# Two decoder layers on one core: other places for the scratch, for w1 and w2 between the layers, and for the kept quarters of V and K

## The chip, the core and the metric

The kernel runs on one core of one Trainium2 chip. TensorE multiplies matrices into PSUM, VectorE, ScalarE and GpSimd work element by element, and SyncE issues the transfers from HBM to SBUF. The metric is the device time of one launch in microseconds. Seen from the profiler, the span runs from the first to the last instruction; the time of the same execution holds a little more.

## The reference

Two times in turn, an attention layer and an MLP are applied to one token x of 512 numbers, with the same weights and the same cache both times:

```
x = x + attention(layernorm(x))     # q = x @ wq, 32 heads of 128, 4096 cached keys and values each
x = x + gelu(layernorm(x) @ w1 + b1) @ w2 + b2      # 512 -> 1376 -> 512, tanh form of gelu
```

All is float32. The scores are q k / sqrt(128), then a softmax over 4096 positions, then the sum of the values, and wo brings 4096 numbers back to 512. K and V take 67 MB each, so nearly all the time's traffic is K and V, read once for each layer.

## The kernel before

**Groups and blocks.** Four heads at a time make a group; there are G = 8 groups, called heads below where the code counts g or n. One group's K, or its V, is a block of 8 MB: 128 partitions x 8 chunks (C) of NC = 2048 numbers, a chunk being four quarters of U = 512. Layer one goes through g = 0 to 7; layer two goes back from g = 7 to 0 (n = 0 to 7), because the last blocks of layer one are still in SBUF when it starts: K and V of g = 7 whole, V of g = 6 in part.

**SBUF.** One tensor, arena, holds everything large, and the code places each piece by its first column:

- Three homes of a whole block each, at A_AT = 0, C_AT = 8 NC and B_AT = 16 NC. In layer one block number 2g (K) and 2g + 1 (V) takes home A, B, C in turn. In layer two, from n = 2 on, the order of homes is A, C, B.
- SHARED, which begins inside home B behind the kept quarters of V (26 of 32) and reaches beyond it: wq at the start, w1 and w2 between the layers, and some of K at the start of layer two.
- SCRATCH, one quarter: the exponentials p of a head, and in head_out the turned copy of the values' sums (ot).
- PAIR, two chunks: wo of this group and wq of the next.

**One head.** scores (64 products of 128 x 512 into pS, one block of K), exponentials (maximum, then ScalarE's exp into SCRATCH), weights (four transposes of p by TensorE, L208, and the denominators), values (64 products into pO, one block of V), head_out (VectorE's transpose L227 into SCRATCH, the reduction L231 that reads it, then the product with wo), next_queries (the product with wq of the next group). The group's share of the attention output is added up in acc.

**Kept quarters.** At g = 6 the last six quarters of V are copied to the PSUM banks pK0 to pK5 by ScalarE as they are used; the other 26 stay in home B. In layer two they are copied back, two to the end of home C and four to PAIR, once those places are free, and V of g = 6 isn't loaded again. K of g = 6 is loaded again in pieces (begin_k), into SHARED, PAIR and home C as they come free.

**Order.** load() puts every transfer on SyncE and keeps it in program order, as matmul() does on TensorE. VectorE, ScalarE and GpSimd are ordered by the tile framework. The framework also adds the waits: an instruction that writes a region of arena waits for those ahead of it in the program that read or wrote an overlapping region. A load so waits on SyncE, and the loads behind it wait with it. A load takes one of eight semaphores in turn, so it also waits for the load eight places ahead of it.

**Between the layers.** The last head of layer one loads its V in four pieces (LAST), then wo, three columns of w1, and behind head_out the fourth. mlp multiplies the four columns into pO, and loads w2 (11 blocks of a quarter) in four pieces as places come free; idle() issues products of zeros that add nothing to the result. Then first_queries begins layer two.

**After that** each head of layer two loads its K, its V (that of n = 2 as five and three chunks) and its pair of weights.

The lines that the change touches:

Of the kernel before, what the change touches and what calls it, by code (L numbers as in the profile page):

```python
# [17 lines left out]
P = 128  # L18
# [3 lines left out]
G = 8  # L22
J = 4
C = 8
FJ = F // J
FB = 11
W1C = FJ * J
EPS = 1e-5
U = 512
# [3 lines left out]

RING = (0, 16 * NC, 8 * NC)
A_AT, B_AT, C_AT = RING
KEPT_V = 26 * U
SHARED = B_AT + KEPT_V
SCRATCH = SHARED + 10 * U  # L40
PAIR = SHARED + 11 * U
ARENA = PAIR + 2 * NC
HALVES = ((0, 4), (4, 8))
W1_AT_END = ((0, 2), (2, 3), (3, 4))
LAST = ((0, 4), (4, 6), (6, 7), (7, 8))
W2_AT_CHANGE = ((0, 2), (2, 5), (5, 8), (8, 11))
W2_AT_END = ((0, 4), (4, 8), (8, 10), (10, 11))


# [1 line left out]
def decode_layers(ctx: ExitStack, tc: tile.TileContext, x, k, v, w, w1, b1, w2, b2, out):  # L51
# [13 lines left out]
    def at(first, n):  # L65
        return arena[:, first : first + n]
# [6 lines left out]
    def matmul(*a, **kw):  # L73
        tc.keep_in_program_order(nc.tensor.matmul(*a, **kw))  # L74
# [53 lines left out]
    def pairs(t):  # L128
        return t[:, :8].rearrange("p (c i) -> p c i", i=2)
# [27 lines left out]
    def minus_mean(s, at):  # L157
        for j in range(J):
            matmul(at[32 * j : 32 * j + 32, :], negmean, s, start=True, stop=True)
        return at  # L160

    def mean_of(xs, s):
        nm = minus_mean(s, pS[:, 0:1])
        xc, sq, ss, negm = small("xc", 4), small("sq", 4), small("ss"), small("negm")
        nc.vector.tensor_scalar(xc, pairs(xs)[:, :, 0], nm, None, op0=ALU.add)
        nc.vector.scalar_tensor_tensor(sq, xc, 1.0, xc, op0=ALU.mult, op1=ALU.mult, accum_out=ss)
        nc.vector.tensor_copy(negm, nm)
        return negm, ss

    def rstd_of(ss):  # L170
        nv = minus_mean(ss, pS[:, 1:2])
        ve, r = small("ve"), small("rstd")
        nc.vector.tensor_scalar(ve, nv, -1.0, EPS, op0=ALU.mult, op1=ALU.add)
        nc.vector.memset(pS[:, 0:2], 0.0)
        nc.gpsimd.tensor_tensor(r, ve, power, op=ALU.pow)
        return r

# [44 lines left out]
            matmul(pO[32 * j : 32 * j + 4, :], pt[:, j, c, :], vt[j],  # L222
                   start=(i == 0), stop=(i == C - 1))

    def head_out(rl, wt, last=False):
        ot = at(SCRATCH, U)
        nc.vector.transpose(ot, pO)  # L227
        o, on = small("o", 4), on_wide
        own = at(SCRATCH, 4 * 129).rearrange("p (b q) -> p b q", q=129)[:, :, :P]
        own = own.rearrange("p b (d q) -> p d b q", q=32)[:, :, :, 0]  # L230
        nc.vector.tensor_reduce(o, own, axis=AX.X, op=ALU.add)  # L231
        if last:
            nc.vector.tensor_scalar(on[:, :4], o, rl, None, op0=ALU.mult)
        else:
            nc.vector.tensor_scalar(in_quarters(on, 4), o.unsqueeze(1).to_broadcast([P, J, 4]), rl, None,  # L235
                                    op0=ALU.mult)
        for d in range(4):
            if last:
                for j in range(J):
                    matmul(pS[32 * j : 32 * j + 1, :P], on[:, d : d + 1], wt[:, d, P * j : P * (j + 1)],  # L240
                           start=(d == 0), stop=(d == 3))
            else:
                matmul(pO, on[:, d : d + P], wt[:, d, :], start=(d == 0), stop=(d == 3))
        return of_32(turned(pS) if last else turned(pO, wide=True), 4)

    def mlp(xs, s, w1_t, w2_t, load_w2=None):
        xb = small("xb", 4)
        nc.gpsimd.tensor_tensor(xb, pairs(xs)[:, :, 0], b2c, op=ALU.add)  # L248
        for c in range(4):
            for j in range(J):  # L250
                matmul(pO[32 * j : 32 * j + 2, :FJ], pairs(xs)[:, c, :], w1_t[c][:, FJ * j : FJ * (j + 1)],
                       start=(c == 0), stop=(c == 3))
            if c == 0:
                nm, ss = mean_of(xs, s)
            if c == 1:
                r = rstd_of(ss)
            if load_w2 and c < 3:
                load_w2(c)
        idle(pS)
        ht = at(SCRATCH, 32 * FB)  # L260
        nc.vector.transpose(ht, pO[:, : 32 * FB])
        h, u, a, z, t, g = (small(f"gelu_{i}", FB) for i in "huaztg")
        nc.vector.scalar_tensor_tensor(h, of_32(ht, FB, 1), nm, of_32(ht, FB), op0=ALU.mult, op1=ALU.add)
        if load_w2:
            load_w2(3)
        nc.vector.scalar_tensor_tensor(u, h, r, b1c, op0=ALU.mult, op1=ALU.add)
        nc.vector.scalar_tensor_tensor(a, u, 0.044715, u, op0=ALU.mult, op1=ALU.mult)
        nc.vector.scalar_tensor_tensor(z, a, 1.0, u, op0=ALU.add, op1=ALU.mult)
        nc.scalar.activation(t, z, AF.Tanh, scale=float(np.sqrt(2.0 / np.pi)))
        nc.vector.scalar_tensor_tensor(g, t, 1.0, u, op0=ALU.add, op1=ALU.mult)  # L270
        for c in range(FB):
            for j in range(J):
                matmul(pS[32 * j : 32 * j + 1, :P], g[:, c : c + 1], w2_t[c][:, P * j : P * (j + 1)],
                       start=(c == 0), stop=(c == FB - 1))
            if load_w2 and any(c == b - 1 for a, b in W2_AT_CHANGE):
                idle(pO)
        return of_32(turned(pS), 4), xb

    def load_w1(first, a, b):
# [33 lines left out]
    def add_up(acc, own):  # L313
        t = small("acc", 4)
        nc.vector.scalar_tensor_tensor(t, own, 1.0, acc, op0=ALU.mult, op1=ALU.add)
        return t


    negm, z, sc, nsc = first_queries(xs, s, wq_t)
    acc = pairs(xs)[:, :, 0]  # L320
    for g in range(G):
        final = g == G - 1
        k_home, v_home = RING[2 * g % 3], RING[(2 * g + 1) % 3]
        for c, t in blocks(k, g, k_home, HALVES if final else ((0, C),)):
            scores(z, c, t)
        pt, rl = weights(exponentials(sc, nsc))
        for c, t in blocks(v, g, v_home, LAST if final else ((0, C),)):
            values(c, pt, t, c)
            if final and c > 4:
                idle(pS)  # L330
            if g == G - 2:
                for j in range(J):
                    i = 4 * c + j - KEPT_V // U
                    if i >= 0:
                        nc.scalar.copy(pK[i], t[j])
        if final:
            wo_t = by_four(load(PAIR, of_w(g % 2, g, 1)))
            for i in range(3):
                load_w1(SHARED, i, i + 1)
            own = head_out(rl, wo_t, last=True)  # L340
            load_w1(SHARED, 3, 4)
        else:
            pair = load(PAIR, of_w(g % 2, g, 2))
            acc = add_up(acc, head_out(rl, by_four(pair[:, :NC])))
            wq_t = by_four(pair[:, NC:])
            z = next_queries(g + 1, xs, negm, wq_t)
    x1, s1 = set_x(own, 1.0, acc, queries=False)
    own, xb = mlp(x1, s1, in_rows(SHARED, W1C, 4), in_rows(SHARED, U, FB),
                  lambda i: load_w2(SHARED, *W2_AT_CHANGE[i]))
    xs, s = set_x(own, 0.5, xb)  # L350


# [2 lines left out]
    g = G - 2  # L355
    negm, z, sc, nsc = first_queries(xs, s, wq_t)
    acc = pairs(xs)[:, :, 0]
    wq_t = by_four(load(SHARED, of_w((g + 1) % 2, g, 1)))
    k_t = []

    def begin_k(home, n):
# [1 line left out]
        load(home, k[g][:, U * a : U * (a + n)])  # L363
        k_t.extend(at(home + U * i, U) for i in range(n))

    begin_k(SHARED + NC, 4)
    begin_k(SHARED + 2 * NC, 2)
    begin_k(PAIR + NC, 4)
    for c in range(C):
        scores(z, c, quarters(C_AT + NC * c))  # L370
# [1 line left out]
            begin_k(C_AT + NC * c, 4)  # L372
        if c == 5:
            begin_k(C_AT + 2 * NC, 14)
    pair = load(C_AT + 22 * U, of_w(g % 2, g - 1, 2))
    p = exponentials(sc, nsc)
    z = next_queries(1, xs, negm, wq_t)
    pt, rl = weights(p)
# [1 line left out]
        values(c, pt, quarters(A_AT + NC * c), c)  # L380
    acc = add_up(acc, head_out(rl, wo_t))

    v_t = [at(B_AT + U * i, U) for i in range(KEPT_V // U)]
    for i, first in enumerate([C_AT + 30 * U, C_AT + 31 * U] + [PAIR + U * j for j in range(4)]):
        t = at(first, U)
        nc.scalar.copy(t, pK[i])
        v_t.append(t)
    for c in range(C):
        scores(z, c, k_t[4 * c : 4 * c + 4])
    pt, rl = weights(exponentials(sc, nsc))  # L390
# [6 lines left out]
    for n in range(2, G):  # L397
        g, final = G - 1 - n, n == G - 1
        k_home, v_home = homes[(2 * n - 1) % 3], homes[2 * n % 3]
        for c, t in blocks(k, g, k_home, HALVES if final else ((0, C),)):  # L400
            scores(z, c, t)
        pt, rl = weights(exponentials(sc, nsc))
        for c, t in blocks(v, g, v_home, LAST if final else ((0, 5), (5, 8)) if n == 2 else ((0, C),)):
            values(c, pt, t, c)
            if final and c > 4:
                idle(pS)
        if final:
            wo_t = by_four(load(PAIR, of_w(g % 2, g, 1)))
            for a, b in W1_AT_END:
                load_w1(A_AT, a, b)  # L410
            for a, b in W2_AT_END:
                load_w2(A_AT + 11 * U, a, b)
            own = head_out(rl, wo_t, last=True)
        else:
            pair = load(PAIR, of_w(g % 2, g - 1, 2))
            acc = add_up(acc, head_out(rl, by_four(pair[:, NC:])))
            z = next_queries(n + 1, xs, negm, by_four(pair[:, :NC]))
# [47 lines left out]
```

## Time and profile before

| | |
|---|---|
| Median of 3 runs | 680.82 us (680.7 to 681.85) |
| Profiled execution, time | 679.55 us |
| Profiled execution, span | 677.8 us |
| Mean granted clock of TensorE | 0.841 |
| Read from HBM | 286.14 MB, 422 GB/s over the span |
| TensorE products, busy | 433.1 us (64%) |
| VectorE, busy | 110.7 us (16%) |
| ScalarE, busy | 22.2 us (3%) |
| GpSimd, busy | 4.3 us (1%) |

In the profile, PE is TensorE, DVE VectorE, ACT ScalarE, POOL GpSimd, SPq the list of SyncE, which is never counted as busy. L74 is the line of matmul(), L70 that of load(), so groups there are told apart by the names behind them: pS<-arena,zq are scores, pO<-arena,turned values. A line of the chain of waits holds start, duration and what it was; a line of a timeline start, duration, engine, line, operation, names, count, and in brackets the idle time before it and what ended it. A line of load issues holds the count, the size of one and the median time from issue to landing; a size isn't printed where it is 8 MB.

### The profile page before, as it was taken

The numbers are of one execution on the slowest core, as the hardware profiler recorded it, in microseconds if no ns is written. First come the engines' busy times: TensorE is split into PE (matmuls) and PEld (weight loads), VectorE is DVE, ScalarE is ACT, GpSimd is POOL, SyncE is SP. The second block draws the span as 40 slices with busy tenths as digits, with TensorE's granted clock in tenths as the row PEclk, the third lists the DMA queues.
The fourth block names the chain that finished last, engine by engine and source line by source line (L and its number), as shares of the span: only waits on it lengthen the run. The fifth ranks groups of instructions, "written<-read, shape, count | busy, mean of one in ns | idle before, by whom it ended". The sixth has DMA issues, their size and how long they took to land. (4 is left out here: it accounts for less than half of the span.)

```text
span 677.8 us, 6359 instructions
## 1 busy us (share of the span) xinstructions
PE 433.1 (64%) x2792; PEld 119.4 (18%) x2792; DVE 110.7 (16%) x431; ACT 22.2 (3%) x47; POOL 4.3 (1%) x21
## 2 busy tenths in 40 slices
PE   1547666485554874667777897686455764766776
PEld 0112112121111211111113222221111111211112
DVE  1012101111021101210212312211021011210211
ACT  0010000000000000001000110000000000000000
POOL 1000000000000000000000000000000000000000
PEclk9969768797698876977979998998698776977977
DMA  9999999999999999999999999899999999999997
GB/s 372 434 433 433 435 433 433 416 449 437 430 433 413 451 433 430 433 431 422 428 413 359 426 459 414 358 468 441 427 433 398 465 433 423 437 430 410 426 416 294
DMA packets 11404, 286.56 MB, mean 423 GB/s; under 512 B 1776, under 2 KB 1776, under 8 KB 3440
## 3 DMA queue, kind: packets, MB, share of 16 engines
q1 hardware_dynamic: 10944, 286.14, 98.7%
q8 instruction: 22, 0.36, 0.2%
q10 hardware_dynamic: 432, 0.01, 0.0%
q14 instruction: 6, 0.05, 0.0%
HBM read 286.14 MB, written 0.00 MB: 422 GB/s over the span
## 5 line engine op out<-in xcount | busy, mean ns | idle before, releaser
L74 PE MATMUL pO<-arena,turned 128*4 128x512 f32 x1024 | 144.8, 726 | 76.8 <-DMA arena<-in_v 75.6
L74 PE MATMUL pS<-arena,zq 128*8 128x512 f32 x1024 | 137.7, 698 | 70.8 <-DMA arena<-in_k 65.4
L74 PE MATMUL pO<-arena,x_wide 128*128 128x512 f32 (+1 forms) x176 | 54.9, 508 | 24.4 <-DVE turned L137 18.1
L74 PE MATMUL pO<-arena,on_wide 128*128 128x512 f32 x112 | 51.8, 605 | 18.6 <-DVE on_wide L235 18.6
L74 PEld LDWEIGHTS pS<-arena,zq 128*8 128x8 f32 x1024 | 29.1, 99 | 176.3 <-issue 167.1
L74 PEld LDWEIGHTS pO<-arena,turned 128*4 128x4 f32 x1024 | 27.6, 97 | 183.8 <-issue 179.5
L137 DVE STREAM_TRANSPOSE turned<-pO 32x128 f32<-32x128 f32 x112 | 35.0, 312 | 101.1 <-PE pO L74 99.9
L227 DVE STREAM_TRANSPOSE arena<-pO 128x512 f32<-128x512 f32 x16 | 11.5, 717 | 220.4 <-PE pO L74 220.4
L208 PE MATMUL pO<-ident,arena 128*128 128x128 f32 x64 | 14.5, 368 | 43.9 <-ACT arena L203 42.4
L196 DVE TENSOR_REDUCE ml<-pS 128x1 f32<-128x512 f32 x16 | 11.1, 692 | 185.0 <-PE pS L74 185.0
L74 PEld LDWEIGHTS pO<-arena,x_wide 128*128 128x128 f32 (+1 forms) x176 | 21.6, 155 | 57.1 <-DVE turned L137 26.5
L203 ACT ACTIVATE arena<-pS,mt,sc 128x512 f32<-128x512 f32 x16 | 12.4, 777 | 523.7 <-DVE mt L201 523.7
L74 PEld LDWEIGHTS pO<-arena,on_wide 128*128 128x128 f32 x112 | 20.1, 189 | 51.7 <-DVE on_wide L235 31.6
L208 PEld LDWEIGHTS pO<-ident,arena 128*128 128x128 f32 x64 | 9.3, 181 | 58.6 <-ACT arena L203 51.3
L74 PE MATMUL pO<-arena,x 128*2 128x344 f32 x64 | 7.2, 531 | 5.0 <-DMA arena<-in_w 4.4
L74 PE MATMUL pS<-arena,zero 128*128 128x512 f32 x16 | 9.9, 706 | 0.0
L74 PE MATMUL pS<-arena,gelu_g 128*1 128x128 f32 x176 | 6.7, 290 | 1.5 <-DVE gelu_g L270 1.3
L213 DVE STREAM_TRANSPOSE mt<-ml 128x32 f32<-128x32 f32 x16 | 3.4, 212 | 17.2 <-ACT arena L203 17.2
L74 PEld LDWEIGHTS pS<-arena,gelu_g 128*1 128x1 f32 x176 | 3.9, 88 | 7.4 <-DVE gelu_g L270 3.7
L211 DVE COPY turned<-pO 128x128 f32<-128x128 f32 x16 | 4.4, 277 | 3.1 <-PE pO L208 3.1
L74 PE MATMUL pO<-arena,zero 128*128 128x512 f32 x8 | 4.5, 644 | 0.0
L248 POOL TENSOR_TENSOR xb<-x,b2c 128x4 f32<-128x4 f32 x2 | 0.4, 200 | 636.9 <-DVE x L148 636.9
(71 smaller groups left out, 76.5 us busy)
## 6 DMA issues: line engine op xcount, KB each, us to landing
arena<-in_w SPq DMA_DIRECT2D x13, 2048.0 KB, 28.8
arena<-in_k SPq DMA_DIRECT2D x4, 4096.0 KB, 42.5
arena<-in_v SPq DMA_DIRECT2D x2, 4096.0 KB, 47.6
arena<-in_w SPq DMA_DIRECT2D x6, 1024.0 KB, 20.3
arena<-in_v SPq DMA_DIRECT2D x1, 5120.0 KB, 23.8
arena<-in_w SPq DMA_DIRECT2D x6, 688.0 KB, 30.2
arena<-in_v SPq DMA_DIRECT2D x2, 2048.0 KB, 50.8
arena<-in_v SPq DMA_DIRECT2D x4, 1024.0 KB, 53.3
```

The lines of the kernel that those rows point to most:

```text
L74: tc.keep_in_program_order(nc.tensor.matmul(*a, **kw))
L137: nc.vector.transpose(t[q], src[q, P * j : P * (j + 1)])
L196: nc.vector.tensor_reduce(ml[:, 0:1], pS, axis=AX.X, op=ALU.max)
L203: nc.scalar.activation(p, pS, AF.Exp, bias=bias[:, 0:1], scale=sc, accum_out=ml[:, 0:1])
L208: tc.keep_in_program_order(nc.tensor.transpose(pT[:, b].rearrange("p j r -> p (j r)"), p[:, P * b : P * (b + 1)], ident))
L211: nc.vector.tensor_copy(pt, pT[:, :, :, :C].rearrange("p b j c -> p j c b"))
L213: nc.vector.transpose(lt, ml)
L227: nc.vector.transpose(ot, pO)
L248: nc.gpsimd.tensor_tensor(xb, pairs(xs)[:, :, 0], b2c, op=ALU.add)
```

## The change

SHARED begins a quarter later, since 27 quarters of V of g = 6 stay in home B and one quarter of K of g = 6 is kept too; five quarters of V and that quarter of K go to the six PSUM banks. The room from SHARED to PAIR is 10 quarters instead of 11. SCRATCH is now the fifth of them. The last head_out of layer one has a place of its own, LAST_OT. In mlp the first product goes into pS and the sums of the layer norm into pO, the other way round than before; the fourth column of w1 takes the place of the first after its products, and one block of w2 is loaded ahead of that column; the other ten follow in four pieces. One idle product stands later, three others are shorter or stand at other blocks. In layer two wq, the pieces of K, the two kept quarters that go to home C, and the pair of weights take other places there, and the third V is loaded as six and two chunks.

```diff
+KEPT_V, KEPT_K = 27, 1
+SHARED = B_AT + KEPT_V * U
+SCRATCH = SHARED + 4 * U
+LAST_OT = SHARED + 3 * W1C
+PAIR = SHARED + 10 * U
-KEPT_V = 26 * U
-SHARED = B_AT + KEPT_V
-SCRATCH = SHARED + 10 * U
-PAIR = SHARED + 11 * U
...
-W2_AT_CHANGE = ((0, 2), (2, 5), (5, 8), (8, 11))
+W1_AT_CHANGE = (0, W1C, 2 * W1C, 0)
+W2_AT_CHANGE = ((0, 1, 9 * U), (1, 3, 3 * U), (3, 7, 5 * U), (7, 10, 0), (10, 11, 3 * U))
...
-    def mean_of(xs, s):
-        nm = minus_mean(s, pS[:, 0:1])
+    def mean_of(xs, s, bank=pS):
+        nm = minus_mean(s, bank[:, 0:1])
...
-        nv = minus_mean(ss, pS[:, 1:2])
+        nv = minus_mean(ss, bank[:, 1:2])
...
-    def head_out(rl, wt, last=False):
-        ot = at(SCRATCH, U)
+    def head_out(rl, wt, last=False, place=SCRATCH):
+        ot = at(place, U)
...
-                matmul(pO[32 * j : 32 * j + 2, :FJ], pairs(xs)[:, c, :], w1_t[c][:, FJ * j : FJ * (j + 1)],
+                matmul(pS[32 * j : 32 * j + 2, :FJ], pairs(xs)[:, c, :], w1_t[c][:, FJ * j : FJ * (j + 1)],
                        start=(c == 0), stop=(c == 3))
             if c == 0:
-                nm, ss = mean_of(xs, s)
+                nm, ss = mean_of(xs, s, pO)
+                if load_w1:
+                    load_w1(3)
             if c == 1:
-                r = rstd_of(ss)
-            if load_w2 and c < 3:
+                r = rstd_of(ss, pO)
+            if load_w2 and 0 < c < 3:
                 load_w2(c)
-        idle(pS)
-        ht = at(SCRATCH, 32 * FB)
-        nc.vector.transpose(ht, pO[:, : 32 * FB])
+        ht = at(SHARED, 32 * FB)
+        nc.vector.transpose(ht, pS[:, : 32 * FB])
...
         if load_w2:
             load_w2(3)
+        idle(pS)
...
-            if load_w2 and any(c == b - 1 for a, b in W2_AT_CHANGE):
-                idle(pO)
+            if load_w2 and c == 1:
+                load_w2(4)
+            if load_w2 and c in (2, 6, 9, 10):
+                idle(pO, U if c < 4 else U // 2)
...
+    def w1_at_change(c):
+        load(SHARED + W1_AT_CHANGE[c], w1[:, W1C * c : W1C * (c + 1)])
+
+    def w2_at_change(i):
+        a, b, first = W2_AT_CHANGE[i]
+        load(SHARED + first, w2[:, U * a : U * b])
...
+        if g == G - 2:
+            for i in range(KEPT_K):
+                nc.scalar.copy(pK[4 * C - KEPT_V + i], t[J - KEPT_K + i])
...
-                    i = 4 * c + j - KEPT_V // U
+                    i = 4 * c + j - KEPT_V
...
-            for i in range(3):
-                load_w1(SHARED, i, i + 1)
-            own = head_out(rl, wo_t, last=True)
-            load_w1(SHARED, 3, 4)
+            for c in range(3):
+                w1_at_change(c)
+            own = head_out(rl, wo_t, last=True, place=LAST_OT)
+            w2_at_change(0)
...
-    wq_t = by_four(load(SHARED, of_w((g + 1) % 2, g, 1)))
+    wq_t = by_four(load(SHARED + 5 * U, of_w((g + 1) % 2, g, 1)))
...
-    begin_k(SHARED + NC, 4)
-    begin_k(SHARED + 2 * NC, 2)
+    def back(i, first):
+        t = at(first, U)
+        nc.scalar.copy(t, pK[i])
+        return t
+
+    begin_k(SHARED, 4)
+    begin_k(SHARED + 9 * U, 1)
     begin_k(PAIR + NC, 4)
...
             begin_k(C_AT + 2 * NC, 14)
-    pair = load(C_AT + 22 * U, of_w(g % 2, g - 1, 2))
+            k_t.append(back(5, C_AT + 22 * U))
+    pair = load(C_AT + 6 * NC, of_w(g % 2, g - 1, 2))
...
-    v_t = [at(B_AT + U * i, U) for i in range(KEPT_V // U)]
-    for i, first in enumerate([C_AT + 30 * U, C_AT + 31 * U] + [PAIR + U * j for j in range(4)]):
-        t = at(first, U)
-        nc.scalar.copy(t, pK[i])
-        v_t.append(t)
+    v_t = [at(B_AT + U * i, U) for i in range(KEPT_V)]
+    v_t += [back(i, C_AT + 23 * U if i == 0 else PAIR + U * (i - 1)) for i in range(4 * C - KEPT_V)]
...
-        for c, t in blocks(v, g, v_home, LAST if final else ((0, 5), (5, 8)) if n == 2 else ((0, C),)):
+        for c, t in blocks(v, g, v_home, LAST if final else ((0, 6), (6, 8)) if n == 2 else ((0, C),)):
```

More of the change, by code (lines that the diff above doesn't have):

```diff
@@ L168, in mean_of, with rstd_of @@
         return negm, ss
-    def rstd_of(ss):
-        nv = minus_mean(ss, pS[:, 1:2])
+    def rstd_of(ss, bank=pS):
+        nv = minus_mean(ss, bank[:, 1:2])
         ve, r = small("ve"), small("rstd")
         nc.vector.tensor_scalar(ve, nv, -1.0, EPS, op0=ALU.mult, op1=ALU.add)
-        nc.vector.memset(pS[:, 0:2], 0.0)
+        if bank is pS:
+            nc.vector.memset(pS[:, 0:2], 0.0)
         nc.gpsimd.tensor_tensor(r, ve, power, op=ALU.pow)
@@ L223, in values @@
                    start=(i == 0), stop=(i == C - 1))
-    def head_out(rl, wt, last=False):
-        ot = at(SCRATCH, U)
+    def head_out(rl, wt, last=False, place=SCRATCH):
+        ot = at(place, U)
         nc.vector.transpose(ot, pO)
         o, on = small("o", 4), on_wide
-        own = at(SCRATCH, 4 * 129).rearrange("p (b q) -> p b q", q=129)[:, :, :P]
+        own = at(place, 4 * 129).rearrange("p (b q) -> p b q", q=129)[:, :, :P]
         own = own.rearrange("p b (d q) -> p d b q", q=32)[:, :, :, 0]
@@ L244, in head_out, with mlp @@
         return of_32(turned(pS) if last else turned(pO, wide=True), 4)
-    def mlp(xs, s, w1_t, w2_t, load_w2=None):
+    def mlp(xs, s, w1_t, w2_t, load_w1=None, load_w2=None):
         xb = small("xb", 4)
@@ L347, in decode_layers @@
     x1, s1 = set_x(own, 1.0, acc, queries=False)
-    own, xb = mlp(x1, s1, in_rows(SHARED, W1C, 4), in_rows(SHARED, U, FB),
-                  lambda i: load_w2(SHARED, *W2_AT_CHANGE[i]))
+    own, xb = mlp(x1, s1, [at(SHARED + first, W1C) for first in W1_AT_CHANGE],
+                  [at(SHARED + first + U * i, U) for a, b, first in W2_AT_CHANGE for i in range(b - a)],
+                  w1_at_change, w2_at_change)
     xs, s = set_x(own, 0.5, xb)
```

## The prediction

> **What bounds the kernel now.** I read the page first, then the chain of waits in order of time, then SyncE's own timeline, its waits and the landing times of single loads. The page:
>
> ```profile
> span 677.8 us, 6359 instructions
> DMA  9999999999999999999999999899999999999997
> HBM read 286.14 MB, written 0.00 MB: 422 GB/s over the span
> ```
>
> The transfers are busy in almost every slice: the end is set by a stream of loads, and what costs time is any moment in which the next load is not queued. The chain of waits shows one head of the second layer (pieces left out between):
>
> ```profile
> 460.20 47.76 DMA arena<-in_k
> ...
> 508.09 8.99 PE pS L74 x64
> ...
> 519.77 0.66 PE pO L208 x4
> 520.43 6.88 another core or an unknown queue
> ...
> 527.44 9.56 PE pO L74 x64
> ...
> 537.77 0.19 DVE o L231
> ...
> 547.47 47.70 DMA arena<-in_k
> ```
>
> K of head n = 4 lands at 460.20 + 47.76 = 507.96. Its 64 score products follow, then the softmax chain, and the four transposes of L208, which read the exponentials p, end at 520.43. V lands at 520.43 + 6.88 = 527.31 (the unnamed piece is the wait for it), 19.35 us after K: that is one 8 MB block on an unbroken stream. The values' products follow, and L231, the reader of head_out's turned copy, ends at 537.96. The pair of wq and wo is a quarter of a block, 4.84 us, so the next K lands 24.2 us after V. When were these loads issued?
>
> ```profile
> 473.12 0.33 SPq L70 DMA_DIRECT2D arena<-in_v  x1
> 503.11 0.33 SPq L70 DMA_DIRECT2D arena<-in_w  x1
> 503.49 0.42 SPq L70 DMA_DIRECT2D arena<-in_k  x1
> 517.10 0.33 SPq L70 DMA_DIRECT2D arena<-in_v  x1
> ```
>
> V of n = 4 at 473.12, 35 us before K ahead of it had landed; K of n = 5 at 503.49, 24 us before its predecessor V landed. This lead keeps the stream unbroken. All loads go through one list on SyncE in program order.
>
> **The step that decides: where SCRATCH now lies.** The ring's home B is B_AT to B_AT + 32U. Before, SCRATCH = B_AT + 26U + 10U = B_AT + 36U, past home B. Now it is B_AT + 27U + 4U = B_AT + 31U, exactly B's last quarter. Every head still writes p there and reads it at L208, and every head_out but layer one's last (which has LAST_OT; layer two's last keeps SCRATCH) writes its turned copy there and reads it at L231. A load of a whole block into B must therefore wait for the readers that stand ahead of it in program order. That such an overlap is kept by region shows in the old kernel's change of layers, where the last column of w1 overlaps the old SCRATCH:
>
> ```profile
> SPq L70 <- DVE o L231: 23.3, 1, 23.3
> 356.09 11.60 SPq L70 DMA_DIRECT2D arena<-in_w  x6
> ```
>
> (SyncE's waits from 343 to 357 us, and its issue right after.) By the order of the homes, B takes V0, K2, V3, K5, V6 in layer one, and K(3), V(4), K(6), V(7) in layer two. A V in B is issued after weights() of its own head, so after its own K has landed and been used; a K in B after head_out of the head before, so after that V has landed and been used. Behind the waiting load on SyncE stand the pair of weights and the next head's K and V, which must go after it. The trace before has no such wait, but it has a restart of an empty queue, at the third V:
>
> ```profile
> 406.36 22.77 SPq L70 DMA_DIRECT2D arena<-in_v  x2
> 429.24 0.37 SPq L70 DMA_DIRECT2D arena<-in_w  x1
> 429.65 0.43 SPq L70 DMA_DIRECT2D arena<-in_k  x1
> ...
> arena<-in_v SPq DMA_DIRECT2D x1, 3072.0 KB, 9.8
> arena<-in_w SPq DMA_DIRECT2D x1, 2048.0 KB, 14.9
> arena<-in_k SPq DMA_DIRECT2D x1, 34.7
> ```
>
> The 3 MB piece was issued at 429.13 - 0.33 = 428.80 and took 9.8 us; 3/8 of 19.35 is 7.26, so a restart costs 2.5 us from issue beyond the bytes. It landed at 438.6, w at 444.1 and K at 464.35: 5.5 and 20.2 us later where an unbroken stream takes 4.84 and 19.35. So the stream loses another 1.6 us in the 35 us after a restart. Why, I do not know; I take 1.3 per restart, between 0 and 2.
>
> The Trainium skill (DMA: Bandwidth & Descriptors, section Anatomy of one DMA) gives another price: some 2.0 us fixed for a transfer beside its bytes, fitted on GpSimd's path. By it, an estimate, eight restarts would come 4 us cheaper; the row of this kernel, 2.5 us, decides.
>
> **Price of a V in B.** From K's landing to the end of L208 the row above gives 520.43 - 507.96 = 12.5 us. Two other heads:
>
> ```profile
> 25.39 9.65 PE L74 MATMUL pS<-arena,zq 128*8 128x512 f32 x64 [17.05 <-DMA arena<-in_k]
> 39.16 1.08 PE L208 MATMUL pO<-ident,arena 128*128 128x128 f32 x4 [4.11 <-ACT arena L203]
> 157.91 9.95 PE L74 MATMUL pS<-arena,zq 128*8 128x512 f32 x64 [5.85 <-DMA arena<-in_k]
> 170.60 1.12 PE L208 MATMUL pO<-ident,arena 128*128 128x128 f32 x4 [2.74 <-ACT arena L203]
> 8.35 0.33 SPq L70 DMA_DIRECT2D arena<-in_v  x1
> arena<-in_v SPq DMA_DIRECT2D x1, 37.6
> ```
>
> Products start 0.13 after the landing, so the head at 157.78 needs 171.72 - 157.78 = 13.9 us, and the first 40.24 - 25.26 = 15.0. I take 13.3 for V3, V6 and V(4), and 15.0 for V0. With 0.1 for SyncE and 2.5 for the restart, V then lands 13.3 + 0.1 + 2.5 = 15.9 us later than on the stream. V0 would land at 40.24 + 0.1 + 2.5 + 19.35 = 62.2; it landed at 8.35 + 37.6 = 46.0: **16.2 us**. The others: 3 x 15.9 = **47.7 us**. V(7) goes in four pieces, and only the last covers quarter 31:
>
> ```profile
> 638.88 3.62 PE L74 MATMUL pS<-arena,zq 128*8 128x512 f32 x32 [0.28 <-DMA arena<-in_k]
> 645.23 1.11 PE L208 MATMUL pO<-ident,arena 128*128 128x128 f32 x4 [2.73 <-ACT arena L203]
> 658.60 1.04 PE L74 MATMUL pO<-arena,turned 128*4 128x512 f32 x8
> ```
>
> Its p is read 7.5 us after K landed, while the seven chunks ahead of it take 7/8 of 19.35, 16.9 us: nothing. Without that cover it would cost some 10 us like the others. The loads of wo, w1 and w2 queued behind it still have 10 us in hand.
>
> **Price of a K in B.** V lands, values, turned copy, L231: 537.96 - 527.31 = 10.65 us, and 0.05 + 2.5 to the restart, 13.2 in all, of which the pair's 4.84 us of transfer covers a part: 8.3 us late. K2, K5 and K(6): **24.9 us**.
>
> **K(3), the change of layers, and the third V.** K(3) is released by L231 of head n = 2, which no load bounds from the first queries of layer two on:
>
> ```profile
> 358.04 0.76 PE L74 MATMUL pO<-arena,x 128*2 128x344 f32 x8 [0.64 <-DVE x L148]
> 362.18 0.76 PE L74 MATMUL pO<-arena,x 128*2 128x344 f32 x8 [0.93 <-DMA arena<-in_w]
> 371.57 0.16 DVE L148 SCALAR_TENSOR_TENSOR x_wide<-turned,xb 128x4 f32<-128x4 f32 x1
> 394.39 0.33 SPq L70 DMA_DIRECT2D arena<-in_k  x1
> arena<-in_k SPq DMA_DIRECT2D x1, 23.7
> 410.19 8.46 PE pO L74 x64
> 450.46 0.19 DVE o L231
> ```
>
> x_wide at 371.57 leads to L231's end at 450.65. Then K(3) lands at 450.65 + 0.05 + 2.5 + 19.35 = 472.55, where it landed at 464.35: **8.2 us**. What shifts x_wide adds to that. Column 3 of w1 is now issued after column 0's products, at 358.8 and not at 356.09, so it lands near 358.8 + 2.5 + 1.6 = 362.9 (1.6 is 688 KB at the stream's rate): 0.8 us after the 362.18 at which its products started. Blocks 7 to 9 of w2, behind gelu_h as before, move by the same amount; part of it is taken up by the shorter idle products. I take **0.5 us**, between -0.5 and 1.5.
>
> The third V matters little. Its six-chunk load covers C_AT + 23U, where quarter 27 of the kept V now lies, so it waits for chunk 6 of the values: 410.19 + 7/8 x 8.46 = 417.6, where K ahead of it lands at 394.39 + 23.7 = 418.1. That is a stall of some 2 us instead of the one at 428.80, and V would still be there near 440 against values that start at 441.5. Both the saved stall (up to 2.7 us: 1.1 in the 3 MB piece and 1.6 behind it) and the saved quarter of K (19.35/32 = 0.6 us) end ahead of K(3), which waits for compute anyway: nothing. The copies to and from PSUM remain 12, on an engine with 22.2 us of work.
>
> **Sum.** 16.2 + 47.7 + 24.9 + 8.2 + 0.5 = 97.5 us. The loss after restarts: eight restarts, one of which replaces the old one: 7 x 1.3 = 9.1. On the profiled execution's 679.55 us (span 677.8 and 1.75 around it): 786.2. The median before is 680.82, 1.3 above the profiled run, so I forecast **787 us**.
>
> **Rivals.** (1) Only V's waits bite, if what is queued ahead of a K covers its wait. The pair alone is 4.84 us against 13.2, so this speaks against itself; it would take off 24.9 + 8.2 and three restarts' 3.9: 750 us. (2) TensorE idles longer and each burst runs at half the pace. 64 products took 7.10 us in the densest stretch and 9.65 after 17 us of idling, no more than the 9.95 after 5.85 us, which speaks against it. At 14.2 instead of 9.6, seven waits grow by 4.6: 819 us. It decides only if an idle time over 17 us does what 17 do not.
>
> ```profile
> 430.35 7.10 PE pS L74 x64
> ```
>
> The Trainium skill (TensorE: Matmul & The Clock Gate, Part 1) has half the clock after idling, but for some 3.4 us of work only. By it, an estimate, a burst is 7.1 + 1.7 = 8.8 us and the sum about 5 us lower; the rows at 9.65 and 9.95 go slightly further, and I keep them.
>
> (3) On the other side: the scratch's readers do not hold the loads, because the order on SyncE lets the blocks into B go as early as before. It decides if V(4)'s issue stays ahead of K(4)'s landing. Then what is left is -0.6 for the quarter, -2.7 for the old third-V stall, +2.5 for the six-chunk load's own restart and 0.5 at the change of layers: 680.5 us, not slower; 678 if the six chunks go in time. The wait on L231 at 356 us speaks against it.
>
> **How the numbers follow.** Forecast 0.83, rival 1 0.06, rival 2 0.05, rival 3 0.05, anything else 0.01. A measurement of this kernel can tell 0.2%, about 1.4 us. All but rival 3 are far slower; rival 3 is split between same and faster. The range: all bursts at 7.1 us (-2.5 on seven waits) and no loss after restarts (-9) give 760; 15.0 us at every V, and 2 us after each restart, give 797. The ends together are less likely than a mixture: 766 to 800.
>
> **What would show it.** SyncE waits on L208 four times and on L231 four times for some 10 us and more; the issue of V(4) comes about 12.5 us after K(4)'s landing; the page's DMA line has eight dips and its mean falls to some 365 GB/s. Bytes fall by 0.26 MB. Wrong if blocks into B are issued ahead of the scratch's readers, or if the span grows by less than 60 us.

## The result, and the profile after

The changed kernel takes 788.93 us (median of 6 runs, 786.61 to 791.59) against 680.76 us before in the same comparison: 1.1586 times as long, 95% interval 1.1558 to 1.1613. The forecast was 787 us. Its profiled execution has a span of 785.3 us, 107.5 more than before.

The page of the changed kernel, the lines that answer to those shown of before:

```profile
span 785.3 us, 6362 instructions
DMA  9299959992999599929999898969982999699997
HBM read 285.88 MB, written 0.00 MB: 364 GB/s over the span
```

The bytes fell by one quarter, 0.26 MB. The line of transfers, nearly all nines before, has the eight holes: four deep ones of 2, which by their times are V0, V3, V6 and V(4), and four lesser ones of 5 and 6 for K2, K5, K(3) and K(6). What SyncE waited for, in the changed kernel (L214 is the old L208, L237 the old L231; behind the colon the total in us, the count and the longest wait):

```profile
SPq L75 <- PE pO L214: 306.9, 6, 70.2
...
SPq L75 <- DVE o L237: 127.3, 4, 36.9
```

The transposes of p and the reader of ot now hold the list of loads for 434 us together. The waits on L214 are six, not four: beside V0, V3, V6 and V(4) it holds the last chunk of V(7) and a column of w1, both with time to spare. The chain of waits of the changed kernel, through one V and one K in home B (pieces left out):

```profile
584.30 4.69 another core or an unknown queue
...
589.13 9.47 PE pS L79 x64
...
601.29 1.13 PE pO L214 x4
602.42 0.02 SPq L75
602.47 0.33 SPq L75
602.85 0.42 SPq L75
603.32 46.68 DMA arena<-in_k
...
669.49 8.55 PE pO L79 x64
...
678.82 0.19 DVE o L237
679.01 0.02 SPq L75
679.06 0.33 SPq L75
```

K(4) lands at 584.30 + 4.69 = 588.99. L214 ends at 602.42, and only then SyncE issues V(4), where the old kernel issued it 35 us ahead of K(4)'s landing. The pair and K(5) go out right behind it: they had stood in the same list. Further on, K(6) goes out when L237 has ended. The chain is no longer transfers one behind another, but transfer, compute, transfer. The landing times of those two loads, counted from their issue:

```profile
arena<-in_v SPq DMA_DIRECT2D x1, 22.5
arena<-in_k SPq DMA_DIRECT2D x1, 22.3
```

With the bytes' 19.35 us taken off, a restart costs 3.1 and 2.9 us. The loss by place, from the issue and landing times of both kernels:

| Load into B | landed before | landed after | late by | added here | predicted, with 1.3 for the restart before it |
|---|---|---|---|---|---|
| V0 | 46.0 | 62.7 | 16.7 | 16.7 | 16.2 |
| K2 | 113.9 | 139.8 | 25.9 | 9.3 | 9.6 |
| V3 | 177.1 | 218.7 | 41.6 | 15.7 | 17.2 |
| K5 | 245.0 | 297.1 | 52.1 | 10.5 | 9.6 |
| V6 | 308.1 | 375.6 | 67.5 | 15.4 | 17.2 |
| K(3) | 464.4 | 544.9 | 80.5 | 13.0 | 10.0 |
| V(4) | 527.3 | 625.0 | 97.6 | 17.1 | 17.2 |
| K(6) | 595.2 | 701.3 | 106.1 | 8.5 | 9.6 |
| end of span | 677.8 | 785.3 | 107.5 | 1.4 | 0 |

### The profile page after: what moved, and what is told of

It reads as the page before. It is cut to its first block, busy times and chain, and to the rows that moved or that the text cites. A ratio compares the mean times of both kernels' runs of the same rounds, so it can differ in the third digit from the quotient of the medians.

```text
span 785.3 us, 6362 instructions
## 1 busy us (share of the span) xinstructions
PE 431.7 (55%) x2792; PEld 119.5 (15%) x2792; DVE 110.6 (14%) x429; ACT 22.3 (3%) x47; POOL 4.3 (1%) x21
## 4 chain that ended last, share of the span: by engine, by line
DMA 51%; PE 34%; DVE 6%; another core or an unknown queue 5%; issue 2%; ACT 1%; SPq 1%; ACTq 0%
DMA arena<-in_k 27%; DMA arena<-in_v 21%; PE pO L79 19%; PE pS L79 14%; DMA arena<-in_w 3%; PE pO L214 1%; DVE turned L142 1%; ACT arena L209 1%; SPq L75 1%; DVE arena L233 1%; DVE ml L202 1%; DVE mb L206 0%; DVE mt L204 0%; DVE mt L207 0%
## 5 line engine op out<-in xcount | busy, mean ns | idle before, releaser
L214 PE MATMUL pO<-ident,arena 128*128 128x128 f32 x64 | 14.3, 364 | 43.9 <-ACT arena L209 42.3
L214 PEld LDWEIGHTS pO<-ident,arena 128*128 128x128 f32 x64 | 9.1, 179 | 58.5 <-ACT arena L209 51.2
L79 PE MATMUL pS<-arena,x 128*2 128x344 f32 x64 | 6.4, 489 | 5.4 <-DMA arena<-in_w 4.7
L219 DVE STREAM_TRANSPOSE mt<-ml 128x32 f32<-128x32 f32 x16 | 3.4, 212 | 17.2 <-ACT arena L209 17.2
L389 ACT COPY arena<-pK 128x512 f32<-128x512 f32 x6 | 3.4, 587 | 30.4 <-PE pO L79 15.5
## 6 DMA issues: line engine op xcount, KB each, us to landing
arena<-in_v SPq DMA_DIRECT2D x2, 4096.0 KB, 51.6
```

Of the source, the lines that this page charges most:

```text
L214: tc.keep_in_program_order(nc.tensor.transpose(pT[:, b].rearrange("p j r -> p (j r)"), p[:, P * b : P * (b + 1)], ident))
L219: nc.vector.transpose(lt, ml)
```

## The experiments

**The scratch past home B.** The changed kernel, SCRATCH one quarter on; two pieces of layer two change places with it.

```diff
-SCRATCH = SHARED + 4 * U
+SCRATCH = SHARED + 5 * U
-    wq_t = by_four(load(SHARED + 5 * U, ...
+    wq_t = by_four(load(SHARED + 6 * U, ...
-    begin_k(SHARED + 9 * U, 1)
+    begin_k(SHARED + 4 * U, 1)
```

> The changed kernel with SCRATCH one quarter further on, just past home B (wq and one quarter of K of layer two give way to it); all else of the change stays. Theory A, the scratch in B's last quarter holds the loads: the eight waits go, and what is left is what the change does between the layers. The changed kernel's K(2) lands 69.3 us after V7, 65.1 before, and the six-chunk load is issued late; with an unbroken stream behind it K(3) would land 115.9 us after V7 and not 111.4: 680.8 + 4.6 = 685 us (682 to 688). Rival, other parts of the change (the late column of w1, the third V, the fewer places) carry half or more of the 108 us: 735 us or above.

Measured: 684.09 us against 680.29, 1.0051 times (1.0031 to 1.0071). Its page:

```profile
span 683.3 us, 6363 instructions
DMA  9999999999999999999998997999999999999997
```

Of the 108 us, 104 were one constant. The nines are back, but for a slice or two at the change of layers and the third V: there the rest of the change still costs 3.8 us.

**The scratch alone, in the old kernel.** p and ot each got a place as an argument; ot of the last head of layer one, and p and ot of the first two of layer two, keep the old place, since SHARED is in use there. (p of the last head of layer one does go to the new place, as in the changed kernel, though the expectation counts it out.)

```diff
+IN_RING = SHARED + 5 * U
-    def exponentials(sc, nsc):
+    def exponentials(sc, nsc, place=IN_RING):
-        p = at(SCRATCH, U)
+        p = at(place, U)
-    def head_out(rl, wt, last=False):
-        ot = at(SCRATCH, U)
+    def head_out(rl, wt, last=False, place=IN_RING):
+        ot = at(place, U)
```

> The old kernel with one thing of the change alone: p and ot of all heads but the last of layer one and the first two of layer two go to B's last quarter, B_AT + 31U. Theory A: the same eight waits as in the changed kernel, 97.0 us and 1.3 for each of seven restarts: 787 us (780 to 791), L208 and L231 four times each ahead of a load into B. Rival: well below, under 735 us.

Then the same with only p there, and with only ot there (the other default set back to SCRATCH):

> As the run with both in the ring, but ot keeps its old place and only p lies in B's last quarter. Theory A, the two sorts of waits add up: only V0, V3, V6 and V(4) wait, 16.2 + 47.7 and 4 x 1.3 after the restarts: 750 us (745 to 755). Rival, one sort alone makes the whole loss since the other is hidden behind it: 787 or 681 us.

> As the run with both in the ring, but p keeps its old place and only ot lies in B's last quarter. Theory A: only K2, K5, K(3) and K(6) wait, 24.9 + 8.2 and 3 x 1.3: 718 us (712 to 722). Rival, the pair of weights covers a K's wait: 681 us.

Measured: 785.72 us with both (1.1537 times, 1.1504 to 1.1569), 749.01 with p alone (1.1006, 1.0977 to 1.1035), 716.70 with ot alone (1.0532, 1.0506 to 1.0559). The transfers' lines of the three pages, in this order:

```profile
DMA  9299959992999599928999999959982999699997
```

```profile
DMA  9289999992899999919999999899982999999997
```

```profile
DMA  9999969999999599999999998789999995999996
```

The first shows both sorts of holes. The second keeps the deep ones, a V behind its own head's p; the third keeps the shallow ones, a K behind ot of the head before, where the pair's transfer fills a part. The sorts add up: 68.7 and 36.4 make 105.1, both together 105.4. So neither hides the other, and rival 1 falls.

**The last chunk loaded apart.** The changed kernel with the scratch where it is, and blocks into B as two loads.

```diff
+TAIL = ((0, 7), (7, 8))
-    ... HALVES if final else ((0, C),)):
+    ... HALVES if final else TAIL if k_home == B_AT else ((0, C),)):
```

(and the same for v_home)

> The changed kernel, scratch still in B's last quarter; every block into home B that is loaded in one piece is loaded as seven chunks and one. Theory A, the wait belongs to the load that covers quarter 31 and to nothing else: the first seven chunks go ahead as before, 16.9 us of stream, and the readers of the scratch come 13.3 us after K or 10.7 us after V, so every wait is covered: about the time with the scratch past home B, 684 us (681 to 688). Rival, the loss comes from sharing the home as a whole, or from something that the position of the scratch only goes along with: 780 us or above.

Measured: 686.67 us, 1.0092 times before (1.0070 to 1.0115). SyncE's waits and the transfers' line of this run (L215 is the transposes, L238 the reader of ot):

```profile
DMA  9999999999999999999997998999999999999997
...
SPq L76 <- PE pO L215: 252.4, 6, 51.6
SPq L76 <- DVE o L238: 130.7, 4, 37.8
```

SyncE still waits 383 us for the same readers, and the waits cost next to nothing: seven chunks of stream cover them. It is not waiting that costs, but waiting with an empty queue. It took 2.6 us more than the first run, by medians from different comparisons; the profiled executions of the two, 685.28 and 685.19 us, do not show the difference, and where it comes from stays open.

**The third V.** In the first run quarter 27 of V still lies in the six-chunk load's way. Here it goes elsewhere:

```diff
-... C_AT + 23 * U if i == 0 else PAIR + U * (i - 1)
+... SHARED + 6 * U if i == 0 else PAIR + U * (i - 1)
```

> The run with the scratch past home B, and quarter 27 of V copied back to SHARED + 6U (free after next_queries(1)) instead of C_AT + 23U, so that the six-chunk load waits for the scores of the second head alone. Theory: the stall at the third V, seen as V issued at 421.6 with K landed at 421.3, goes; K(3) lands near 465 and not at 469.5: 680 us (678.5 to 682). Rival, the time lost between the layers sets K(3) anyway: 684 us.

Measured: 681.72 us, 1.0013 times before (1.0002 to 1.0023). SyncE's timeline at that place, with the scratch past B only, and then with quarter 27 moved too:

```profile
396.66 0.33 SPq L75 DMA_DIRECT2D arena<-in_k  x1
421.64 11.22 SPq L75 DMA_DIRECT2D arena<-in_v  x2
```

```profile
396.73 0.33 SPq L75 DMA_DIRECT2D arena<-in_k  x1
408.78 22.59 SPq L75 DMA_DIRECT2D arena<-in_v  x2
```

V goes out 13 us earlier, and K(3) lands 43.7 us after K(2) (421.6 to 465.3) instead of 48.2 (421.3 to 469.5). The time lies near the upper end of what was expected, 678.5 to 682 us.

**The third V alone, in the old kernel.**

```diff
-    pair = load(C_AT + 22 * U, ...
+    pair = load(C_AT + 24 * U, ...
-    ... [C_AT + 30 * U, C_AT + 31 * U] + [PAIR ...
+    ... [SHARED, SHARED + U] + [PAIR ...
-    ... ((0, 5), (5, 8)) if n == 2 ...
+    ... ((0, 6), (6, 8)) if n == 2 ...
```

> The old kernel with only the idea of the third V, and without its wait: pair at C_AT + 24U, quarters 26 and 27 of V copied back to their own places in SHARED after next_queries(1), V(2) as six and two chunks. Theory: the old stall (1.1 us in the 3 MB piece and 1.6 behind it) goes and nothing comes in its place: 680.3 - 2.7 = 677.6 us. Rival, the stream's lag comes back within the next loads anyway: 679.5 to 680.5 us.

Measured: 680.11 us against 681.08, 0.9987 times (0.9975 to 0.9999). The step in the trace is as expected, K(3) 43.7 us after K(2) and 46.3 before, but only 1.0 of 2.7 us reached the end. A window between the layers, in the old kernel and then in this run (the granted clock third from the end):

```profile
362.00:368.00 6.00, 4.74 (x54) 1.83 (x54) 1.52 (x6) 0.21 (x1) 0.00 (x0) 1.00 0.95 376
```

```profile
362.00:368.00 6.00, 5.53 (x52) 1.74 (x52) 1.53 (x6) 0.21 (x1) 0.00 (x0) 0.72 0.99 364
```

Its profiled execution took 682.03 us, the longest of its twelve: the clock was down here, K(2) landed 2.8 us later, and K(3) no earlier than before. That accounts for this execution; where the median loses its part isn't shown.

**Idle products ahead of the late column.** Two products of zeros in the first run, behind column 2 of w1:

```diff
+            if load_w2 and c == 2:
+                idle(pO)
+                idle(pO)
```

> The run with the scratch past home B, and two idle products more between columns 2 and 3 of w1 in layer one, where TensorE now stands still for some 2 us until the late column lands. Theory, the late column costs twice, by the wait and by the slower products behind it: the two last columns' products take 0.76 us again, not 1.3 for the last, the first three blocks of w2 0.85 and not 1.46 us, and the first queries of layer two start about 1 us earlier than 17.1 us after the first column's products. Rival, those products are slow for another reason: no change in them. The whole time moves by under 1 us either way, 683 to 684.5.

Measured: 682.20 us, 1.0019 times before (1.0006 to 1.0031); the run without them had 1.0051. TensorE's timeline without the idle products, then with them (columns 2 and 3 of w1, then the first three blocks of w2):

```profile
360.47 1.33 PE L79 MATMUL pS<-arena,x 128*2 128x344 f32 x8 [0.88 <-DMA arena<-in_w]
362.98 1.33 PE L79 MATMUL pS<-arena,x 128*2 128x344 f32 x8 [1.19 <-DMA arena<-in_w]
...
366.98 1.46 PE L79 MATMUL pS<-arena,gelu_g 128*1 128x128 f32 x24
```

```profile
360.29 0.76 PE L79 MATMUL pS<-arena,x 128*2 128x344 f32 x8 [0.88 <-DMA arena<-in_w]
360.98 1.98 PE L79 MATMUL pO<-arena,zero 128*128 128x512 f32 x4
362.89 0.76 PE L79 MATMUL pS<-arena,x 128*2 128x344 f32 x8
...
365.78 0.84 PE L79 MATMUL pS<-arena,gelu_g 128*1 128x128 f32 x24 [0.34 <-DVE gelu_g L281]
```

(The gap ahead of column 3 is 1.19 us in the run without them; the 2 us of the expectation are the changed kernel's.) The products of column 3 and of the first three blocks of w2 run nearly twice as fast once TensorE isn't left standing. Those of column 2 differ too, though nothing was put ahead of them, so where the clock falls varies with the execution. What doesn't vary: the two products of zeros behind column 3 take 2.07 or 2.08 us in all four profiles of the changed layout without the added ones, and 1.12 us in both with them. The first queries start 16.0 us after the first column's products instead of 17.1, as expected. The expectation that the whole moves by under 1 us was wrong: by the two ratios it is some 2 us. K(2) landed 1.5 us earlier and K(3) 2.8.

**Both repairs together, in the old kernel and in the changed one.** The old kernel with the third V and idle products behind columns 1 and 2 (half an idle product and a whole one):

> The old kernel with the third V as six and two chunks without its wait, and with one and a half idle products more in layer one's mlp, behind columns 1 and 2 of w1, where TensorE waits for the next column. Theory: the third V saves 2.7 us in each execution, and a part of them gives it back between the layers, where the granted clock fell to 0.72 in the profiled one; with the clock kept up the saving stays: 678.5 us (677.5 to 679.5), K(2) landing 65 us after V7 and K(3) 43.7 after K(2). Rival, what is lost between the layers does not hang on the clock: 680 us as without the idle products.

The changed kernel with scratch, quarter 27 and the two idle products repaired:

> The changed kernel with its three costs taken out: scratch past home B, quarter 27 of V in SHARED + 6U, two idle products ahead of the late column of w1. Theory, the costs add up: 681.7 with the first two, less the 1.9 us that the idle products gave alone: 679.8 us (679 to 681), no slower than the old kernel and no more than 0.3% faster. Rival, with the third V unbroken the idle products no longer matter: 681.7 us.

Measured: 680.47 us for the old kernel's version, 0.9990 times before (0.9980 to 1.0000), and 680.39 for the changed one's, 0.9994 (0.9981 to 1.0007). The second is within what was expected. The first misses it by 2 us and came out at its rival's 680 us: the granted clock was 1.00 from 362 to 368 us in its profiled execution, and the gain still didn't come, so the clock there doesn't account for what is lost. In that execution K(2) lands at 418.8 and K(3) 44.7 us later, 1.6 better than before; the last piece of V(7) still lands 0.8 us earlier than before, and the pieces of w1 and w2 behind it take that back, so that the span is even. In the profiled execution of the second, 0.9 us at V(7) become 1.0 at the end. With its costs taken out, the idea of the change is neither faster nor slower than the old kernel within what can be told.

## Why the prediction was right

**The step that decides** held: SCRATCH at B_AT + 31U makes eight loads wait for the readers of p and ot. Moving it out takes 104 of 108 us away, moving it in adds 105, and loading its chunk apart takes 102 away, though not the wait.

**A V in B.** From K's landing to V's issue it was 15.1 us at V0, then 12.1, 12.1 and 13.5 (15.1 and 13.4 predicted). The head chosen as typical was slightly too slow: three V's came to 48.2 us where 51.6 with their restarts were in the sum. V(7)'s last chunk was hidden, as worked out.

**A K in B.** From V's landing to K's issue 11.0, 11.2 and 9.7 us (10.7 predicted); the three came to 28.3 us where 28.8 with their restarts were in the sum.

**A restart.** Mis-sized in two terms that offset each other. From issue to landing beyond the bytes the eight loads took 2.5 to 3.2 us, 2.8 on average, where the sum had 2.5. The five chunks ahead of the row that the 2.5 was read from landed at 406.36 + 23.8 = 430.2, 1.4 us after that issue, so its queue was nearly empty and not quite. Up to the landing of the second block behind it the stream then lost another 0.6 to 1.3 us beyond the bytes, 1.0 on average, in seven of the eight, where the sum had 1.3; behind V6 it was 1.7, but the old kernel loses 1.35 at the same place. The price that the Trainium skill (DMA: Bandwidth & Descriptors, Anatomy of one DMA) gives for another path, 2.0 us, would have been further off. Where the stream loses more can be seen: each load leaves 16 landing events in the trace and counts as landed with the last. First and last lie 0.5 to 1.4 us apart at the eight restarted loads and 1.8 to 2.1 us two blocks later, and for each of the eight this growth, 0.5 to 1.3 us, makes up most of what was lost. Why they drift apart stays open.

**K(3) and the change of layers** are the term that failed: 13.0 us against 10.0. From the last landing of V7 to x_wide it took 20.9 us, 18.6 before: 2.3 and not 0.5. Column 3 landed at 431.07, 4.1 us after its issue, as worked out. But its products began 1.15 us later behind V7's last landing than before, where 0.8 was worked out, and TensorE had stood idle for 2.07 us ahead of them; that they and those behind them would run slower wasn't priced:

```profile
428.28 0.76 PE L79 MATMUL pS<-arena,x 128*2 128x344 f32 x8 [0.51 <-DMA arena<-in_w]
431.11 1.32 PE L79 MATMUL pS<-arena,x 128*2 128x344 f32 x8 [2.07 <-DMA arena<-in_w]
433.11 2.07 PE L79 MATMUL pS<-arena,zero 128*128 128x512 f32 x2 [0.67 <-DVE arena L268]
```

(TensorE in the changed kernel; the same eight products took 0.76 us before.) From x_wide to K(3)'s issue another 1.6 us were lost, nearly all in the values of the first head of layer two: the same 64 products, before and after, with the granted clock:

```profile
387.00:396.00 9.00, 7.40 (x65) 1.91 (x66) 1.35 (x4) 0.00 (x0) 0.00 (x0) 1.00 0.98 421
```

```profile
457.00:466.00 9.00, 8.75 (x64) 1.86 (x64) 0.13 (x2) 0.00 (x0) 0.00 (x0) 0.81 0.98 419
```

(Windows of 9 us around them, before and then after: TensorE's busy time stands second, the granted clock third from the end.) Why the clock fell there and not before is open: with the scratch past B, those products took 7.05 us again though the late column was still there:

```profile
389.55 7.05 PE L79 MATMUL pO<-arena,turned 128*4 128x512 f32 x64 [0.38 <-DVE turned L217]
```

K(3)'s own restart took 0.7 us more than the sum had, and the loss behind V6's restart was 1.0 us less than it had, since the old kernel's stream loses most of that too. That the total came within 2 us of the forecast is in part luck: the three V's were 3.4 us too long in the sum, K(3) 3.0 too short, and the last 1.4 us, from K(6) to the end, were put at nothing.

**The third V** cost and saved nothing in the changed kernel, since K(3) waits for compute, as argued. What it would cost alone was right in kind (K(3) 48.2 us after K(2)) and the old stall's worth was overrated: of 2.7 us, 0.5 and 1.0 reached the end in the two old-kernel runs, with intervals that go down to nothing.

**The rivals.** Rival 1 falls with the two single runs. Rival 2 falls by the trace: bursts of 64 products after 20 us and more of standing still took 8.5 to 9.8 us, no more than before. The longest and one of the shortest, in the changed kernel:

```profile
62.80 9.76 PE L79 MATMUL pO<-arena,turned 128*4 128x512 f32 x64 [22.55 <-DMA arena<-in_v]
625.09 8.51 PE L79 MATMUL pO<-arena,turned 128*4 128x512 f32 x64 [22.69 <-DMA arena<-in_v]
```

The 22 bursts of 64 products that waited for a load average 9.2 us, between the rows of the prediction at 9.6 and the 8.8 us that it estimated from the Trainium skill (TensorE: Matmul & The Clock Gate, Part 1). Rival 3, a kernel no slower, is what the scratch past home B nearly gives; in the changed kernel the condition it named, V(4) issued ahead of K(4)'s landing, did not come.

## What to carry to other kernels

In a kernel that a stream of loads bounds, the place of a small scratch decides when a large load may start: check each constant of the layout against every buffer of the ring, the last quarter included, and ask for each overlap which reader stands ahead of which load in program order. A wait on an in-order list of loads holds all that stands behind it, but costs only the time in which the queue is empty; so load the contested part apart and last, and the wait is covered as long as the parts ahead of it take longer (here 16.9 us of stream against waits of 10 to 15 us). When the time of a change is worked out from such a list, take for each load the later of "stream arrives" and "released plus restart", and follow it from one to the next.

## What the runs showed of the hardware

- An emptied queue costs 2.8 us from issue to landing beyond the bytes (2.5 to 3.2, eight restarts of 8 MB loads), and the stream lags by about 1.0 us more some 44 us later, as the 16 landing events of one load spread from 0.5 to 1.4 us to some 2 us.
- Eight products after a gap of 2.07 us ran at 1.32 us instead of 0.76; with products of zeros in such a gap, 0.76 in two runs. The gap alone does not decide: in one of the four profiles without them (the last chunk apart) they ran at 0.76 in spite of a gap of 2.78 us, and what came next was slow; eight others ran at 1.33 after a gap of 0.88 us in one run and at 0.76 after the same gap in another. A late load can so cost its wait and then the slower products behind it.
- Small gains at the change of layers do not reach the end in full: 2.6 and 1.6 us seen between two landings gave 1.0 and 0.5 us of time. How the rest is lost isn't settled.
